# Sliding-window attention into a SiLU MLP: attention in visits of two blocks, and second layers by seven block products

## The chip, the cores and the metric

The kernel runs on one core of a Trainium2 chip. The metric is the device time of one execution in microseconds. The profiled execution is one further run of the same program, taken with the hardware profiler. In its views PE is TensorE's matmul, PEld its weight load, DVE is VectorE, ACT is ScalarE, POOL is GpSimd (here it writes the descriptors of casting loads) and SP is SyncE (here it issues stores and DMA transposes); L12 is line 12 of the kernel.

## What is computed

```python
batch, n_heads, seq, head_dim = (8, 8, 576, 64)
# attention, causal, window of 64
scores = scale * np.matmul(q, k.transpose(0, 1, 3, 2))
mask = (rel >= 0) & (rel < window)            # rel = query position - key position
attn = softmax(np.where(mask, scores, -1e9))
attn_out = np.matmul(attn, v)
x = attn_out.transpose(0, 2, 1, 3).reshape(B * S, H * D)      # 4608 x 512
h = x @ w_in                                  # 512 -> 2048
g = h * (1.0 / (1.0 + np.exp(-h)))
out = g @ w_out                               # 2048 -> 512
```

All inputs and the output are float32; both kernels multiply in bfloat16 and accumulate in float32.

## The kernel before

**Tiling.** A block is 64 query positions of one batch; a block's queries see the 128 keys of their own block and the one before. There are 9 blocks in a batch and 72 in all. A tile of the MLP is 512 tokens, 8 blocks, and there are 9 tiles. `bridge` holds the attention output transposed (model dimension on the partitions), as the first layer wants it. The first layer of a tile is 16 feature groups of 4 matmuls over 512 columns (`first_layer`, L440), each group followed by a SiLU on ACT into a `g` buffer (L446). The second layer is, for each 128 tokens, 16 matmuls over 512 columns into one bank (`second_layer`, L449), a copy to `ot` (L455) and a store by SP (L459). Tile 0's first layer is cut into columns 0 to 191 and 192 to 511; the last 128 tokens of the last tile are cut into 256, 128 and 128 output columns.

**Attention before** goes in units of two heads and three blocks (`add_batch_attention`), 12 to a batch. q is kept as `qbd`, with the two heads of a pair in a block diagonal, so that one matmul of 128 rows and 128 columns gives the scores of a block for both heads (L349, three to a unit). Exp runs on ACT (L367), the mask is a multiplication on DVE (L370; in batch 0 a matmul adds a bias instead, L356), the values are three matmuls of 130 columns (L375), in which a column of ones gives the row sums; reciprocal (L381) and normalisation on DVE follow. The result gets into `bridge` by matmuls back (L420 in batch 0, with 64 output columns that alternate between the halves of the array; L431 in batch 1 and most of 2) and a copy, or from the last third of batch 2 on by a DMA transpose on SP (L425).

**Loads.** POOL issues loads that cast to bfloat16: whole rows for TensorE transposes (L235; the transposes are L299, with 64 output columns in alternating halves, and L308), or pieces of 64 elements for DMA transposes (L254; the transposes are L260). q goes by TensorE in batches 0 to 3, k in 0 and 1. SP loads the first q and k pair itself (L241). v is loaded by L272 and shifted by half a block on DVE (L335, L337). Buffers for k, q and v are double, by batch, so that v of batch b waits until the values of batch b - 2 are done.

**Order.** A planner, `Plan`, sets the order of work on every engine before anything is emitted. Every operation has a cost in microseconds, what it needs, and a rank by its class; DMA operations have a cost on one of two pipes and a latency. The planner steps through time and on each free engine places the ready operation of the lowest rank. The order that comes out is fixed: on the chip, each engine's queue runs in that order, and an operation whose input is late holds up all that is behind it. MLP matmuls have rank 99, so any ready attention matmul goes ahead of them, but scores go only where `scores_may_run` lets them, which is during second layers:

```python
        op, kind, rest = moe[i]
        if kind == 1:
            return rest > 0 and not p.done(op["deps"])
        return rest > 6
```

PSUM has eight banks: four (`at`) for attention, four (`mp`) for the MLP. While the first tile has not begun, filler matmuls (`warm`, L680) go where TensorE would be idle.

Of the kernel before, what the change touches and what calls it, by code (L numbers as in the profile page):

```python
# [14 lines left out]
class Plan:  # L15
# [5 lines left out]
    def __init__(self, pools, rank, rank0, ahead):  # L21
        self.rank, self.rank0, self.pools = rank, {**rank0, **{c + "0": r for c, r in ahead.items()}}, pools
        self.queues = {}
        self.banks = [[] for _ in range(8)]
        self.count = 0
        self.now = 0.0

    def add(self, cls, us, fn, deps=(), lat=0.08, gate=None, dma=None, pool=None, table=None, b=0):
        if b > 1 and cls in ("cast", "lift", "spread", "mask", "norm"):
            lat = 0.2  # L30
        op = dict(us=us, first=self.rank[cls] + b if b or cls not in self.rank0 else self.rank0[cls], fn=fn, deps=[d for d in deps if d is not None], lat=lat, gate=gate, dma=dma,
                  pool=pool, table=table, seen=None, n=self.count, until=[], bank=None)
        self.count += 1
        self.queues.setdefault(cls, []).append(op)
        return op

    def add_filler(self, n, cls, us, fn, *args, **kw):

        for _ in range(n):
            op = self.add(cls, us, None, *args, **kw)  # L40
            op["until"], op["fn"] = [op], lambda e, op=op: fn(op)
        self.count -= n

    def done(self, ops):
        return all(d["seen"] is not None and d["seen"] <= self.now for d in ops)

    def run(self):
# [7 lines left out]
        while left:  # L55
# [6 lines left out]
            while moved:  # L62
                moved = False
                for e in engines:
# [3 lines left out]
                    for c in can[e]:  # L68
# [8 lines left out]
                        if op["pool"] and not any(self.done(self.banks[i]) for i in self.pools[op["pool"]]):  # L77
                            continue
# [4 lines left out]
                    if op["pool"]:  # L83
                        banks = self.banks
                        op["bank"] = min((i for i in self.pools[op["pool"]] if self.done(banks[i])),
                                         key=lambda i: max([u["seen"] for u in banks[i]], default=0.0))
                        banks[op["bank"]] = op["until"]
# [8 lines left out]

# [9 lines left out]
                    heapq.heappush(events, op["seen"])  # L106
        for op, e in order:
# [4 lines left out]
def kernel(ctx, tc, q, k, v, w_in, w_out, out):  # L112
# [8 lines left out]
    NG = 3  # L121
# [5 lines left out]
    NK = 2  # L127
    NN, NNB, NE, NOB, NOT, NGT = 8, 8, 14, 6, 4, NFT + 3
    PARTS = {0: [(0, 192), (192, TT)]}
    NXQ, NXK, NXO = 4, 2, 3  # L130
    NRAW, NOX, NRC = 2, 2, 12
    NIV, NPM = 2, 1
    scale = 1.0 / float(D) ** 0.5

# [7 lines left out]
    twoi = keep.tile([128, 64], BF16, name="twoi")  # L142
    zero = keep.tile([128, NP], FP32, name="zero")
    spare = keep.tile([128, NP], FP32, name="spare")
    window = keep.tile([128, 64], BF16, name="window")
    mask0 = keep.tile([128, 3, 2, 64], BF16, name="mask0")
    mask = keep.tile([128, 3, 2, 64], BF16, name="mask")
    bias0 = keep.tile([128, 3, 2, 64], BF16, name="bias0")
    bias = keep.tile([128, 3, 2, 64], BF16, name="bias")
    nats = [keep.tile([NR, 2, NM, 128], BF16, name=f"nat{i}") for i in range(NN)]  # L150
    natbs = [keep.tile([NR, 2 * NM * D], BF16, name=f"natb{i}") for i in range(NNB)]
    qbd = [keep.tile([128, NP, 2, S], BF16, name=f"qbd{i}") for i in range(NK)]
    kt = [keep.tile([128, 64 + NP * S], BF16, name=f"kt{i}") for i in range(NK)]
    vv = [keep.tile([128, H * NB + 1, D + 2], BF16, name=f"vv{i}") for i in range(NK)]
    es = [keep.tile([128, 3, 2, 64], BF16, name=f"e{i}") for i in range(NE)]
    rcs = [keep.tile([128, 3, 2], FP32, name=f"rc{i}") for i in range(NRC)]
    obs = [keep.tile([128, 3, 128], BF16, name=f"ob{i}") for i in range(NOB)]
    raws = [keep.tile([128, 2, S], BF16, name=f"raw{i}") for i in range(NRAW)]
    oxs = [keep.tile([128, 3, NP, 128], BF16, name=f"ox{i}") for i in range(NOX)]
    gts = [keep.tile([128, TT], BF16, name=f"g{i}") for i in range(NGT)]  # L160
    ots = [keep.tile([128, d_model], FP32, name=f"ot{i}") for i in range(NOT)]
# [3 lines left out]
    banks = [psum.tile([128, 512], FP32, name=f"at{i}") for i in range(4)]  # L165
    banks += [psum.tile([128, 512], FP32, name=f"mp{i}") for i in range(4)]

    p = Plan(
        {"at": range(4), "mp": range(4, 8), "all": range(8)},
        rank=dict(prime=-8, one=-9, first=-9, dma=-1, ld0=-1, ld1=-1, st=-2, xo=-1.5, xk=-1.4, silu=-3, out=-2, pv=0, ot=0, s=1, moe=99, warm=200, turn=2,  # L170
                  norm=0, inverse=0, bridge=0, exp=1, mask=1, lift=2, spread=2, shift=2, cast=4, late=5, clear=9),
        rank0=dict(turn=-6, cast=-6, lift=-5, shift=-4.5, exp=-4, mask=-4, inverse=-3.5, norm=-3, bridge=-3.2),
        ahead=dict(s=-5.5, exp=-4.6, pv=-5.5, inverse=-4.3, norm=-4.2, ot=-5.5, bridge=-4.25),
# [11 lines left out]

# [6 lines left out]
    def const_bias(_):  # L192
        for t in (bias, bias0):
            nc.vector.tensor_copy(out=t.rearrange("p t h i -> p (t h) i"),
                                  in_=window.unsqueeze(1).to_broadcast([128, 6, 64]))
        nc.vector.memset(bias0[0:64, 0], -32768.0)

    def const_mask(_):
        for a, m in ((bias, mask), (bias0, mask0)):
            nc.vector.tensor_scalar(m, a, 1.0 / 32768.0, 1.0, op0=ALU.mult, op1=ALU.add)  # L200

    def const_twoi(_):
        nc.vector.tensor_copy(out=twoi[0:64], in_=ident[0:64, 0:64])
        nc.vector.tensor_copy(out=twoi[64:128], in_=ident[64:128, 64:128])
# [8 lines left out]
    def clear_q(i, hh):  # L213
        r = slice(64 - 64 * hh, 128 - 64 * hh)
        nc.scalar.copy(out=qbd[i][r, :, hh].bitcast(FP32), in_=zero[r].unsqueeze(2).to_broadcast([64, NP, S // 2]))

    def clear_ob(i):
        nc.vector.memset(obs[i].bitcast(FP32), 0.0)

    c_ident = p.add("one", {"POOL": 1.3}, const_ident)  # L220
    c_vv = [p.add("one", {"DVE": 0.25}, lambda _, i=i: clear_vv(i)) for i in range(NK)]
    c_k = [p.add("one", {"DVE": 0.15}, lambda _, i=i: clear_k(i)) for i in range(NK)]
    c_zero = p.add("one", {"DVE": 0.1}, lambda _: nc.vector.memset(zero, 0.0))
    c_q = {i: [p.add("first", {"ACT": 1.0}, lambda e, i=i, hh=hh: clear_q(i, hh), [c_zero]) for hh in range(2)]
           for i in range(NK)}
    c_twoi = p.add("late", {"DVE": 0.3}, const_twoi, [c_ident])
    c_ob = [p.add("late", {"DVE": 0.2}, lambda _, i=i: clear_ob(i)) for i in range(NOB)]
    c_window = p.add("one", {"POOL": 0.6}, const_window)
    c_bias = [p.add("one", {"DVE": 0.9}, const_bias, [c_window])]
    c_mask = [p.add("late", {"DVE": 0.7}, const_mask, c_bias)]  # L230


    def load_cast(w, b, pj, kk):

        nc.gpsimd.dma_start(  # L235
            out=natbs[w].rearrange("p (h y) -> p h y", h=2),
# [499 lines left out]
```

## Time and profile before

| | us |
|---|---|
| median of three runs | 317.87 |
| the three runs | 317.87, 315.54, 319.26 |
| the profiled execution's span | 318.8 |

The span runs from the first to the last instruction of the profiled execution. TensorE's granted clock is 0.995 of full speed on average over it.

How to read what the prediction quotes: the page's second part cuts the span into 40 slices and gives the busy share of each in tenths, and in the row PEclk the granted clock in tenths. Its fourth part is the chain of waits, followed back from the last instruction. A row of the timeline has start, length, engine, line, operation, output and input, the number of instructions that are merged into it, and in brackets the idle time before it with what ended that. Matmuls are pipelined, so a row's length reaches past the start of the next; the distance between starts is what a group costs. A row of the costliest groups has count, total busy time, mean nanoseconds of one, and idle time before with its releasers. A row of the view by stretches has the stretch, its length, the busy time (and count) of PE, PEld, DVE, ACT and POOL, the granted clock, the DMA share and GB/s. A row of DMA issues has count, size, and the median time from issue to landing.

### The profile page before, as it was taken

How to read it: one execution, taken by the hardware profiler on the slowest of the kernel's cores; microseconds unless marked ns; L12 is line 12 of the kernel's file. 1: busy time of each engine (PE TensorE's matmuls, PEld its weight loads, DVE VectorE, ACT ScalarE, POOL GpSimd, SP SyncE). 2: the span in 40 equal slices, each digit the busy share in tenths (PEclk: the TensorE clock that was granted, in tenths of full speed). 3: DMA queues.
4: the chain of work that ended last, by engine and by line, in shares of the span. 5: the costliest groups of instructions: out<-in, count | busy, mean ns of one | idle time of the engine just before them, and what ended most of it. 6: DMA issues, size and time to landing. Idle time of an engine off the chain costs nothing.

```text
span 318.8 us, 6010 instructions
## 1 busy us (share of the span) xinstructions
PE 307.9 (97%) x2198; PEld 168.4 (53%) x2223; DVE 154.5 (48%) x467; ACT 193.4 (61%) x374; POOL 119.2 (37%) x159
## 2 busy tenths in 40 slices
PE   8999999999999999999999869999999999999996
PEld 4778666545664556445544445446544444444444
DVE  4894748934799898923990159606920000000000
ACT  8898786889776565568356721668166126415611
POOL 8947859496829777564454000000000000000000
PEclk9999999999999999999999979999999999999999
DMA  9999999999999999999999933400340020020012
GB/s 144 164 196 186 193 195 161 127 243 129 187 165 135 176 154 152 163 163 163 154 191 175 142 64 90 84 0 36 80 93 2 35 97 0 2 99 33 2 61 70
DMA packets 138108, 37.51 MB, mean 118 GB/s; under 512 B 122464, under 2 KB 133600, under 8 KB 138080
## 3 DMA queue, kind: packets, MB, share of 16 engines
q0 software_dynamic: 95712, 18.06, 74.4%
q1 hardware_dynamic: 42368, 19.08, 33.6%
q8 instruction: 17, 0.28, 0.4%
q14 instruction: 11, 0.09, 0.1%
HBM read 36.70 MB, written 9.44 MB: 145 GB/s over the span
## 4 chain that ended last, share of the span: by engine, by line
PE 85%; DVE 6%; DMA 4%; issue 2%; ACT 1%; POOL 1%; DVEq 0%; POOLq 0%; ACTq 0%
PE mp L449 36%; PE mp L440 32%; PE at L375 5%; PE at L349 4%; DMA vv<-in_v_dram 4%; DVE qbd L314 2%; PE at L680 1%; PE mp L680 1%; DVE ox L404 1%; POOL vv L272 1%; DVE qbd L268 1%; DVE vv L337 1%; DVE vv L335 1%; PE at L308 1%; PE at L420 1%
## 5 line engine op out<-in xcount | busy, mean ns | idle before, releaser
L449 PE MATMUL mp<-w_out_sb,g 128*128 128x512 bf16 (+2 forms) x583 | 141.6, 369 | 1.0
L440 PE MATMUL mp<-bridge,w_in_sb 128*128 128x512 bf16 (+2 forms) x640 | 130.7, 358 | 0.7 <-ACT g L446 0.6
L446 ACT ACTIVATE g<-mp 128x512 bf16<-128x512 f32 (+2 forms) x160 | 86.3, 556 | 29.8 <-PE mp L440 29.3
L440 PEld LDWEIGHTS <-w_in_sb 128*128 128x128 bf16 x640 | 60.1, 98 | 60.3 <-issue 1.4
L449 PEld LDWEIGHTS <-g 128*128 128x128 bf16 x608 | 55.0, 98 | 42.7
L455 ACT COPY ot<-mp 128x512 f32<-128x512 f32 (+2 forms) x34 | 19.0, 561 | 72.1 <-PE mp L449 62.7
L404 DVE TENSOR_TENSOR ox<-at,rc 64x192 bf16<-64x192 f32 x128 | 45.2, 353 | 2.5
L254 POOL DMA_DIRECT2D nat<-in_k_dram x48 | 36.4, 761 | 24.3 <-DMA nat<-in_k_dram 13.0
L367 ACT ACTIVATE e<-at 128x384 bf16<-128x384 f32 x90 | 38.8, 497 | 10.6 <-PE at L349 9.8
L370 DVE TENSOR_TENSOR e<-e,mask 128x384 bf16<-128x384 bf16 x84 | 26.6, 350 | 33.6 <-ACT e L367 32.8
L272 POOL DMA_DIRECT2D vv<-in_v_dram x32 | 32.3, 1014 | 13.1 <-PE at L375 7.2
L375 PE MATMUL at<-vv,e 128*128 128x130 bf16 x273 | 29.8, 220 | 4.1 <-DVE e L370 4.0
L375 PEld LDWEIGHTS <-e 128*128 128x128 bf16 x288 | 22.5, 97 | 20.0 <-DVE e L370 7.6
L254 POOL DMA_DIRECT2D nat<-in_q_dram x32 | 23.4, 735 | 8.1 <-DMA nat<-in_q_dram 4.6
L349 PEld LDWEIGHTS <-kt 128*128 128x128 bf16 x252 | 18.6, 100 | 10.0 <-issue 2.8
L349 PE MATMUL at<-qbd,kt 128*128 128x128 bf16 x252 | 23.6, 222 | 0.3
L381 DVE RECIPROCAL rc<-at 128x6 f32<-128x6 f32 x91 | 17.5, 194 | 10.1 <-PE at L375 8.0
L314 DVE COPY qbd<-at 64x288 bf16<-64x288 bf16 x26 | 12.5, 480 | 11.1 <-ACT qbd L314 7.6
L387 DVE TENSOR_TENSOR ob<-at,rc 64x192 bf16<-64x192 f32 x40 | 14.0, 350 | 0.8
L314 ACT COPY qbd<-at 64x288 bf16<-64x288 bf16 x22 | 10.5, 476 | 2.8 <-DVE qbd L314 2.5
L268 DVE COPY qbd<-raw 64x1152 bf16<-64x1152 bf16 x16 | 8.1, 505 | 8.4 <-DMA raw<-nat 8.0
L235 POOL DMA_DIRECT2D natb<-in_q_dram x15 | 10.0, 665 | 4.9 <-PE at L375 1.4
(69 smaller groups left out, 158.0 us busy)
## 6 DMA issues: line engine op xcount, KB each, us to landing
out_dram<-ot SPq DMA_DIRECT2D x35, 256.0 KB, 2.4
vv<-in_v_dram POOLq DMA_DIRECT2D x32, 144.0 KB, 7.3
nat<-in_k_dram POOLq DMA_DIRECT2D x48, 72.0 KB, 7.9
nat<-in_q_dram POOLq DMA_DIRECT2D x32, 72.0 KB, 7.6
natb<-in_q_dram POOLq DMA_DIRECT2D x15, 144.0 KB, 6.4
w_in_sb<-in_moe_w_in_dram POOLq DMA_DIRECT2D x8, 256.0 KB, 8.7
w_out_sb<-in_moe_w_out_dram POOLq DMA_DIRECT2D x8, 256.0 KB, 7.8
natb<-in_k_dram POOLq DMA_DIRECT2D x7, 144.0 KB, 5.9
```

The lines of the kernel that those rows point to most:

```text
L254: nc.gpsimd.dma_start(out=rows(i)[:, pj % 2, :, 64 * hh:64 * hh + 64], in_=(q, k)[kk][b, 2 * pj + hh].rearrange("(m p) d -> p m d", p=NR),)
L272: queue[e].dma_start(out=vv[b % NK][:, 2 * g0 + 1:2 * g1 + 1:2, 0:D], in_=v[b].rearrange("h s d -> (h s) d").rearrange("(g p) d -> p g d", ...
L314: copies[e](out=qbd[b % NK][64 * hh:64 * hh + 64, pj, hh].rearrange("x (p m) -> x p m", m=NM)[:, :, r::2], in_=at_bf16(op)[64 * r:64 * r + ...
L349: nc.tensor.matmul(at_sp(op)[:, x], lhsT=kt[b % NK][:, pj * S + t * 64:pj * S + t * 64 + 128], rhs=qbd[b % NK][:, pj, :, t * 64:t * 64 + 6 ...
L367: nc.scalar.activation(out=es[n % NE], in_=at_sp(op), func=ACTF.Exp, scale=scale)
L370: nc.vector.tensor_mul(es[n % NE], es[n % NE], mask0 if g == 0 else mask)
L375: nc.tensor.matmul(at_pv(op)[:, x], lhsT=es[n % NE][:, x].rearrange("p h i -> p (h i)"), rhs=vv[b % NK][:, s:s + NB + 1:NB, 0:D + 1], star ...
L404: nc.vector.tensor_mul(ox(n)[:, :, r], pv[r, :, hh, 0:D], rc[r, :, hh:hh + 1].to_broadcast([64, 3, 64]))
L440: nc.tensor.matmul(banks[bank["bank"]][:, lo:hi], lhsT=w_in_sb[:, c, ft * 128:(ft + 1) * 128], rhs=bridge[:, (j * TT + lo) // 64:(j * TT + ...
L446: nc.scalar.activation(out=gts[gt][:, lo:hi], in_=banks[bank["bank"]][:, lo:hi], func=ACTF.Silu)
L449: nc.tensor.matmul(banks[bank["bank"]][:, 0:hi - lo], lhsT=gts[gt][:, m * 128:(m + 1) * 128], rhs=w_out_sb[:, f, lo:hi], start=(f == 0), s ...
L455: copies[e](out=ots[ot][:, lo:hi], in_=banks[bank["bank"]][:, 0:hi - lo])
```

## The change

**Attention.** A visit takes two consecutive blocks and all eight heads (36 visits; a visit may span two batches). q is kept plainly as `qt`, without zeros: a pair's two heads lie on partitions 0 to 63 and 64 to 127 of `qt` and `kt`. Scores are 16 matmuls of 64 rows and 64 columns, which alternate between the row halves and between the two banks of a PSUM pair. Values are 16 matmuls of 65 columns that write 64 partitions each, alternating between column halves. Exp and mask then are one operation over 1024 elements, normalisation one over 512. Two pairs of banks serve scores and values in turn. Visits 0 to 8 go to `bridge` by TensorE transposes and a copy, the others by a DMA transpose each on SP. q and k go by TensorE transposes in batches 0 and 1 and by DMA transposes from batch 2 on, both straight to where they are used; there are seven `nat` buffers. In batch 0 all q and k loads go through POOL ahead of the v loads, and five of the eight `w_out` loads go ahead of batch 1. Tile 0's first layer is cut at column 256.

**Second layers.** Tile 0's stays as it was. From tile 1 on, g (512 tokens x 2048) and w_out (2048 x 512) are each cut into quarters, and the product is formed by seven quarter products instead of eight, in Winograd's form of Strassen's algorithm. Each quarter product is 2 x 8 matmuls of 256 columns. Four sums of quarters of g are formed for each tile on DVE, in two halves each; four sums of quarters of w_out are formed once (`wsum`). Partial products accumulate in the same bank across products, with a copy of the bank to `ot` in between (ACT) or an addition of the bank to `ot` (DVE).

The planner has one rank for each class and one default latency (0.2 in place of 0.08), can hand out pairs of banks, and lets scores run while more than 1.5 us of a second layer is left.

```diff
-    def scores(op, b, pj, g):
-        for x in range(3):
-            t = 3 * g + x
-            nc.tensor.matmul(
-                at_sp(op)[:, x], lhsT=kt[b % NK][:, pj * S + t * 64:pj * S + t * 64 + 128],
-                rhs=qbd[b % NK][:, pj, :, t * 64:t * 64 + 64], start=(x == 0), stop=(x == 2),
-            )
+    def scores(op, blocks, bias):
+        ps = pair(op).rearrange("k (h x j i) -> k h x j i", h=2, x=2, j=NP)
...
+        for x, nb in enumerate(blocks):
+            b, t = divmod(nb, NB)
+            for j in range(NP):
+                for hh in range(2):
+                    r = slice(64 * hh, 64 * hh + 64)
+                    nc.tensor.matmul(
+                        ps[:, hh, x, j], lhsT=kt[b % 2][r, j * S + t * 64:j * S + t * 64 + 128],
+                        rhs=qt[b % 2][r, j * S + t * 64:j * S + t * 64 + 64],
+                        start=(x == 0 and j == 0 and not bias), stop=(x == n - 1 and j == NP - 1),
+                    )
+    def values(op, w, blocks):
...
+                for hh in range(2):
+                    h = 4 * (j // 2) + 2 * hh + j % 2
+                    nc.tensor.matmul(
+                        o[64 * hh:64 * hh + 64, x, j], lhsT=es[w][:, hh, x, j],
+                        rhs=vv[b % 2][:, h * NB + t, 0:D + 1], start=(j == 0), stop=(j == NP - 1),
+                    )
+    def g_sum(i, f0, f1):
+        x, y = {0: (a_quarter(21), a_quarter(22)), 1: (sums[0], a_quarter(11)),
+                2: (a_quarter(11), a_quarter(21)), 3: (a_quarter(12), sums[1])}[i]
+        (nc.vector.tensor_sub if i else nc.vector.tensor_add)(sums[i][:, f0:f1], x[:, f0:f1], y[:, f0:f1])
+    def w_sum(i, f0, f1):
+        x, y = {0: (b_quarter(12), b_quarter(11)), 1: (b_quarter(22), wsum[0]),
+                2: (b_quarter(22), b_quarter(12)), 3: (b_quarter(21), wsum[1])}[i]
+        nc.vector.tensor_sub(wsum[i][:, f0:f1], x[:, f0:f1], y[:, f0:f1])
-    def second_layer(bank, gt, m, f, lo, hi):
-        nc.tensor.matmul(
-            banks[bank["bank"]][:, 0:hi - lo], lhsT=gts[gt][:, m * 128:(m + 1) * 128], rhs=w_out_sb[:, f, lo:hi],
-            start=(f == 0), stop=(f == NFT - 1),
-        )
+    def product(bk, a, w, m, f, first, last):
+        nc.tensor.matmul(
+            bank(bk)[:, HD * m:HD * m + HD], lhsT=a[:, f, 128 * m:128 * m + 128], rhs=w[:, f],
+            start=first and m == 0 and f == 0, stop=last and f == HF - 1, skip_group_check=True)
+    def add_second(j, si, pool):
...
+        for f0 in (0, 4):
+            f1 = f0 + 4
+            need = [x for f in range(f0, f1) for x in si[f] + si[f + HF]]
+            for i in (0, 1, 3, 2):
+                before = {0: [], 1: su[0][-1:], 2: [], 3: su[1][-1:]}[i]
+                su[i].append(p.add("sum", {"DVE": 0.68}, lambda _, i=i, f0=f0, f1=f1: g_sum(i, f0, f1),
+                                   need + before + s_used[i]))
...
+        a, e1 = add_product(None, a_quarter(11), b_quarter(11), lambda f: si[f], True, False, use_g(0))
+        p1 = piece(a, o11, e1, "copy", free(o11))
+        c, e5 = add_product(None, sums[0], wsum[0], lambda f: [su[0][f // 4]] + tsum[0], True, False, use_s(0))
+        p5 = piece(c, o22, e5, "copy", free(o22))
+        _, e6 = add_product(a, sums[1], wsum[1], lambda f: [su[1][f // 4], p1] + tsum[1], False, False, use_s(1))
+        u2 = piece(a, o12, e6, "copy", free(o12))
+        _, e3 = add_product(c, sums[3], b_quarter(22), lambda f: [su[3][f // 4], p5], False, True, use_s(3))
+        c12 = piece(c, o12, e3, "add", [u2])
+        _, e7 = add_product(a, sums[2], wsum[2], lambda f: [su[2][f // 4], u2] + tsum[2], False, False, use_s(2))
+        c22 = piece(a, o22, e7, "add", [p5])
+        bb, e2 = add_product(None, a_quarter(12), b_quarter(21), lambda f: si[f + HF], True, True, use_g(1))
+        c11 = piece(bb, o11, e2, "add", [p1])
+        _, e4 = add_product(a, a_quarter(22), wsum[3], lambda f: si[f + HF] + [c22] + tsum[3], False, True, use_g(1))
```

In the order that comes out of the changed planner, score and value bursts stand in the second layers of tiles 0 to 5 and at the start of tile 2's first layer; tiles 6 to 8 hold none. On DVE the shifts of v stand between masks, normalisations and, in tiles 1, 2 and 4, between the sums of g.

More of the change, by code (lines that the diff above doesn't have):

```diff
@@ L120 @@
     NR = S // NM
-    NG = 3
     NDC = d_model // 128
@@ L149 @@
[L149 to L161, printed above, removed]
+    window0 = keep.tile([128, 64], BF16, name="window0")
@@ L211, in clear_k @@
         nc.vector.memset(kt[i][:, 0:64].bitcast(FP32), 0.0)
[L213 to L218, printed above, removed]
     c_ident = p.add("one", {"POOL": 1.3}, const_ident)
[L221 to L222 removed]
+    c_vv = [p.add("one", {"DVE": 0.25}, lambda _, i=i: clear_vv(i)) for i in range(2)]
@@ L223 @@
+    c_k = [p.add("one", {"DVE": 0.15}, lambda _, i=i: clear_k(i)) for i in range(2)]
     c_zero = p.add("one", {"DVE": 0.1}, lambda _: nc.vector.memset(zero, 0.0))
[L224 to L227, printed above, removed]
     c_window = p.add("one", {"POOL": 0.6}, const_window)
-    c_bias = [p.add("one", {"DVE": 0.9}, const_bias, [c_window])]
```

712 lines of the change are left out of this document (342 added, 370 removed).

## The prediction

> **What bounds the kernel now.** I read the page first, then the instructions in order of time at the end of the run and in its middle.
>
> ```profile
> PE 307.9 (97%) x2198; PEld 168.4 (53%) x2223; DVE 154.5 (48%) x467; ACT 193.4 (61%) x374; POOL 119.2 (37%) x159
> PEclk9999999999999999999999979999999999999999
> DMA  9999999999999999999999933400340020020012
> PE 85%; DVE 6%; DMA 4%; issue 2%; ACT 1%; POOL 1%; DVEq 0%; POOLq 0%; ACTq 0%
> ```
>
> TensorE is busy 97% of the span and carries 85% of the chain of waits; no other engine passes 61%. The DMA engines are full for the first 23 of 40 slices and nearly idle afterwards, so transfers matter only while attention is still being fed. TensorE's time is not in its "mean ns" (matmuls overlap) but in the distance between starts:
>
> ```profile
> 287.85 13.98 PE L440 MATMUL mp<-bridge,w_in_sb 128*128 128x512 bf16 x64
> 301.67 14.06 PE L449 MATMUL mp<-w_out_sb,g 128*128 128x512 bf16 x95
> 301.93 0.60 ACT L446 ACTIVATE g<-mp 128x512 bf16<-128x512 f32 x1 [0.27 <-PE mp L440]
> ...
> 312.27 0.59 ACT L455 COPY ot<-mp 128x512 f32<-128x512 f32 x1 [2.87 <-PE mp L449]
> 314.02 0.37 ACT L455 COPY ot<-mp 128x256 f32<-128x256 f32 x1 [1.16 <-PE mp L449]
> ```
>
> 64 matmuls of 512 columns take 301.67 - 287.85 = 13.82 us, 216 ns each. The copies that follow 16 matmuls of 256 columns lie 314.02 - 312.27 = 1.75 us apart, 109.4 ns each: half the columns cost half the time. The MoE part of before is then 1088 x 0.216 = 235.0 plus tile 0's first layer in two parts, 14.0: 249.0 us. The attention rates:
>
> ```profile
> 27.77 0.42 PE L308 MATMUL at<-ident,natb 96*128 96x96 bf16 x6
> 28.03 0.41 PE L440 MATMUL mp<-bridge,w_in_sb 128*128 128x192 bf16 x3
> 28.37 0.45 PE L299 MATMUL at<-ident,natb 96*64 96x96 bf16 x12
> 28.75 1.65 PE L440 MATMUL mp<-bridge,w_in_sb 128*128 128x192 bf16 x14
> ...
> 46.54 0.25 PE L431 MATMUL at<-twoi,ob 128*128 128x64 bf16 x3
> 46.63 0.38 PE L449 MATMUL mp<-w_out_sb,g 128*128 128x512 bf16 x1
> ...
> 145.34 0.83 PE L349 MATMUL at<-qbd,kt 128*128 128x128 bf16 x12
> 146.01 2.11 PE L449 MATMUL mp<-w_out_sb,g 128*128 128x512 bf16 x8
> ...
> 163.37 0.34 PE L375 MATMUL at<-vv,e 128*128 128x130 bf16 x3
> 163.54 13.76 PE L440 MATMUL mp<-bridge,w_in_sb 128*128 128x512 bf16 x63
> ```
>
> Scores cost 0.67/12 = 56 ns, values 0.17/3 = 57 ns, the matmuls back 30 ns. Batches 1 to 7 hold 252 scores (14.1 us) and 252 values (14.4), 60 backs (1.8), 12 bursts of q transposes (0.26 each, 3.1), and bursts with 64 output columns priced next (3.1): 36.5 us.
>
> ```profile
> 20.38 0.33 PE L361 MATMUL at<-qbd,kt 128*128 128x128 bf16 x3
> 20.64 0.38 PE L420 MATMUL mp<-ident,ox 128*64 128x64 bf16 x12
> 20.95 0.35 PE L375 MATMUL at<-vv,e 128*128 128x130 bf16 x3
> 21.22 0.28 PE L420 MATMUL mp<-ident,ox 128*64 128x64 bf16 x6
> 21.44 0.34 PE L375 MATMUL at<-vv,e 128*128 128x130 bf16 x3
> ```
>
> These L420 matmuls write alternating column halves of the array. Six take 0.22 us, twelve 0.31: six more cost 0.09, 15 ns each, half of L431's 30, so the halves run side by side. The group ahead is stretched too (L361 x3 takes 0.26 where 0.17 is usual). So a burst costs about 0.22 us once, and 64/4.8 = 13 ns per matmul. L299 agrees: 12 x 96/4.8 ns + 0.22 = 0.46; the rows give 0.38, and 0.09 ahead.
>
> Now the span closes: first layer at 22.1 (row below), 249.0, 36.5, and 3.1 from the last matmul to the end make 310.7 of 318.8. The other 8.1 are waits, most of them in one place:
>
> ```profile
> 184.71 0.76 DVE L337 COPY vv<-vv 64x2304 bf16<-64x2304 bf16 x1 [4.52 <-DMA vv<-in_v_dram]
> 185.99 0.51 PE L375 MATMUL at<-vv,e 128*128 128x130 bf16 x3 [4.00 <-DVE e L370]
> 186.00:189.20 3.20, 3.20 (x20) 2.10 (x21) 2.32 (x7) 1.30 (x3) 0.00 (x0) 0.52 0.21 79
> ```
>
> The shift of a late v stood ahead of masks on VectorE; TensorE stood 4.0 us and then ran 3.2 us at a granted clock of 0.52, 1.5 more.
>
> **The change, part by part.** *Second layers.* Tiles 1 to 8 run 7 x 16 products of 256 columns instead of 64 of 512: 112 x 0.1094 = 12.25 against 13.82, so 8 x 1.57 = -12.5 us. Tile 0's first layer, 128 x 0.109 = 14.0, is unchanged. MoE after: 14.0 + 512 x 0.216 + 13.8 + 98.0 = 236.4.
>
> *What the products wait for.* Each tile adds 8 sums and 3 adds on VectorE.
>
> ```profile
> L370 DVE TENSOR_TENSOR e<-e,mask 128x384 bf16<-128x384 bf16 x84 | 26.6, 350 | 33.6 <-ACT e L367 32.8
> L410 DVE TENSOR_TENSOR ox<-at,rc 128x384 bf16<-128x384 f32 x6 | 3.2, 541 | 0.1
> L455 ACT COPY ot<-mp 128x512 f32<-128x512 f32 x31 | 18.1, 586 | 69.8 <-PE mp L449 60.4 <-issue 8.7 <-ACT e L367 0.7
> L381 DVE RECIPROCAL rc<-at 128x6 f32<-128x6 f32 x91 | 17.5, 194 | 10.1 <-PE at L375 8.0 <-ACT ot L455 0.3
> ```
>
> A sum is 1024 bf16 elements; the mask does 384 in 0.35, so at most 0.93 in proportion; I take 0.7, as part of 0.35 is fixed. That is 5.6 us a tile, and 2.2 of adds (3 x 0.541 x 512/384), in a period of 26. The last silu ends 0.9 us after the layer's last matmul (301.93 + 0.60 against 301.67). The second half of the first sum is ready 0.7 later, at 1.6; the first product (1.75 us) needs no sum and the second reaches its fifth block at 2.2. The copy that frees the accumulating bank (0.59) lies beside the product on the other bank (1.75). So nothing waits, with 0.6 us to spare; a VectorE later than that costs TensorE the difference, since all matmuls queue behind the product. VectorE stays near half busy: normalising goes to 36 operations of 0.72 from 168 halves by the code, the qbd copies go.
>
> *Attention.* 32 visits follow tile 0's start, each with 16 scores (64 rows, 64 columns) and 16 values (64 output columns, 65 columns). Values are L420's form: 0.22 + 16 x 0.0135 = 0.44 us. No row shows 64-row scores with halves in rows: 0.43 if they pair like L420, 0.69 at L431's 30 ns. I take 0.50, nearer the first, because q and k halves sit in different partitions and banks. 32 x 0.94 = 30.1, less some 7 bursts that follow one of the same kind (1.5); batch 1's turns, 8 x 0.46, and five visits back, 20 x 0.056, add 4.8: 33.4 against 36.5, -3.1.
>
> *Start and end.*
>
> ```profile
> 2.08 1.11 POOL L272 DMA_DIRECT2D vv<-in_v_dram  x1
> ...
> 9.11 1.03 POOL L272 DMA_DIRECT2D vv<-in_v_dram  x1
> ...
> 17.49 0.32 DVE L337 COPY vv<-vv 64x576 bf16<-64x576 bf16 x1
> 22.12 0.82 PE L440 MATMUL mp<-bridge,w_in_sb 128*128 128x192 bf16 x8
> out_dram<-ot SPq DMA_DIRECT2D x35, 256.0 KB, 2.4
> out_dram<-ot SPq DMA_DIRECT2D x2, 64.0 KB, 1.6
> bridge<-ox SPq DMA_TRANSPOSE x16, 6.2
> kt<-nat SPq DMA_TRANSPOSE x12, 9.2
> ```
>
> Now all eight q/k loads go through POOL ahead of v (SP loads none), and a visit needs all heads. Between the two POOL rows lie two more v issues (1.0) and six q/k issues, 0.65 each, so the last v issue moves to about 2.1 + 8 x 0.65 + 3 x 1.0 = 10.3; 8.4 us later, as from 9.11 to 17.49, its shift starts, 18.7. Values at 19.4, then four normalisations in a row on VectorE (0.19 + 0.72) and the last back: first layer near 24.0, +1.9. At the end the last piece is 512 wide instead of 128: copy 0.59 where 256 columns take 0.37, store 2.4 for 1.6. That is about 1.1 more: 4.2 for 3.1.
>
> *Waits.* Visits from the tenth on reach the bridge by a DMA transpose on SP. Tile 2 needs visit 11, whose values stand only 26 products (2.8) and four bursts (1.8) ahead of tile 2's first matmul. From their start it takes the values 0.44, reciprocal 0.2, a shift 0.4, normalisation 0.72 and a landing of 6.2, about 8, so TensorE waits 3.3, plus 1.4 of half clock (as at 186 us). Behind it in TensorE's queue stands everything. SP now carries 24 q/k and 27 o transposes between the stores, some behind a store that waits for an add; an o transpose that lands late meets this case again, but later tiles take their last blocks a whole tile ahead. The 8.1 us of before: k, q and v of batches 3 and 4 are wanted at about 85 to 115 us, near when they land (kt 9.2 us after issue), and shifts stand between the sums. Between 0 and another 8 to 10; I take 4. Waits: 8.7.
>
> Sum: 24.0 + 236.4 + 33.4 + 8.7 + 4.2 = 306.7 against the profiled execution's 318.8; the median of the three runs, 317.87, lies 0.9 lower, so 305.8.
>
> **Rivals** (each time on the scale of the median). *Row halves don't hide their weight load (slower).* L420 shows only column halves.
>
> ```profile
> L440 PEld LDWEIGHTS <-w_in_sb 128*128 128x128 bf16 x640 | 60.1, 98 | 60.3 <-issue 1.4
> ```
>
> If each 64-row score stood for a whole 98 ns load: 16 x 0.098 + 0.22 = 1.79 a visit, +1.29 x 32 = +41: 347. Halves overlapping, 49 ns: +16, 322. It passes before from 12 us/512 = 24 ns more than my 0.50 allows (18 a matmul): 42 ns. Against it: L431 loads 128 columns and multiplies 64 in 30 ns. The Trainium skill's "TensorE: Matmul & The Clock Gate", in "LDWEIGHTS (loading the stationary operand)", sets a load at columns/1.2, whatever the rows, which is 107 ns here; by that estimate the time would be about 350 unhidden. L431's 30 ns disagrees for full-height loads; no run here shows 64 rows.
>
> *Late transfers in fixed queues.* The price of one is 4.0 + 1.5 as at 182 to 189 us; three beyond my sum give 322, two 317. The full DMA row up to 180 us speaks for it, and so does q of batches 2 and 3, now eight row loads a batch instead of four larger ones; against it, before met it once.
>
> *Sums late.* VectorE 1.4 us late in each of 8 tiles: +11, 317. Against: 48% busy.
>
> *Better.* Scores at 0.43, only tile 2's wait: 305.8 - 2.2 - 4 = 299.6, and with no wait there 294.9.
>
> **How the numbers follow.** Forecast 0.53 (300 to 312); better 0.12; transfers 0.16, half of it within 1% or slower; sums 0.07; row halves 0.12, mostly slower. Within 1% (314.7 to 321) is what a measurement can't tell from no change. Faster 0.53 + 0.12 + 0.08 = 0.73; same 0.05 + 0.07 = 0.12; slower 0.03 + 0.12 = 0.15. The range goes from 295, the better case, to 319, which takes in two late transfers and late sums.
>
> **What would show it.** Right: products start 109 ns apart; score bursts take 0.4 to 0.7 us; first layer near 24; a wait of some 3 us on the o transpose ahead of tile 2. Wrong: score starts over 42 ns apart, products waiting for VectorE in most tiles, or TensorE idle over 15 us after 24.

## The result and the profile after

| | us, median (lowest to highest) | executions |
|---|---|---|
| the changed kernel | 326.31 (325.95 to 328.63) | 4 |
| the kernel before, on the same chip | 316.71 (315.34 to 319.26) | 4 |

The ratio is 1.0295, with a 95% interval from 1.0212 to 1.0379: the change made the kernel 3% slower. The forecast was 305.8, faster. The profiled execution took 325.95, with a span of 324.2. The executions of a kernel fall into a shorter and a longer group; the ratios here and below compare the shorter ones alone, and the profiled execution of the kernel before (its span of 318.8 stands for a time of some 320.6, as a time lies 1.7 to 1.9 above its span in every run) is one of the longer.

The page of the changed kernel, its first, second and fourth part:

```profile
PE 297.5 (92%) x3052; PEld 190.9 (59%) x3056; DVE 139.8 (43%) x263; ACT 169.9 (52%) x263; POOL 125.2 (39%) x169
...
PEclk9999999999996799999979999999999999999999
DMA  5999999999999999999979999900530120030003
...
PE 57%; DMA 22%; issue 8%; POOL 5%; ACT 4%; DVE 2%; POOLq 0%; ACTq 0%; DVEq 0%
```

TensorE has 10 us less work than before (297.5 against 307.9), as meant, but a span that is 5 longer. It carries 57% of the chain of waits instead of 85%, and DMA 22% instead of 4%. What TensorE waited for, in the view of waits (engine and line, what it waited for, us in total, times, longest):

```profile
PE mp L367 <- DMA bridge<-ox: 5.0, 1, 5.0
PE at L305 <- DMA qt<-nat: 3.8, 2, 3.1
PE at L367 <- ACT gt L373: 3.0, 4, 0.7
PE at L400 <- ACT ot L612: 2.0, 3, 0.7
...
PE at L400 <- DVE ot L613: 1.2, 1, 1.2
```

Two are late transfers: a transposed attention output (`bridge`) and a transposed q. The other three are on `at`, the attention's PSUM banks, and were in no part of the forecast. The timeline of TensorE tells where each lies (start, length, instruction, idle time before and its releaser):

```profile
27.62 10.97 PE L367 MATMUL mp<-bridge,w_in_sb 128*128 128x256 bf16 x99 [0.29 <-DVE bridge L362]
...
47.09 0.64 PE L305 MATMUL at<-qt,kt 64*128 64x64 bf16 x32
47.66 2.55 PE L396 MATMUL mp<-w_out_sb,gt 128*128 128x512 bf16 x10
...
103.52 4.00 PE L367 MATMUL mp<-bridge,w_in_sb 128*128 128x512 bf16 x9 [4.95 <-DMA bridge<-ox]
107.45 0.65 PE L335 MATMUL at<-vv,e 128*64 128x65 bf16 x16
...
162.57 0.47 PE L305 MATMUL at<-qt,kt 64*128 64x64 bf16 x20 [3.06 <-DMA qt<-nat]
...
248.27 1.91 PE L400 MATMUL mp<-w_out_sb,gt 128*128 128x256 bf16 x16
...
260.50 13.98 PE L367 MATMUL mp<-bridge,w_in_sb 128*128 128x512 bf16 x64
...
286.54 1.24 PE L367 MATMUL at<-bridge,w_in_sb 128*128 128x512 bf16 x5
288.53 1.89 PE L367 MATMUL at<-bridge,w_in_sb 128*128 128x512 bf16 x8 [0.75 <-ACT gt L373]
...
303.98 1.91 PE L400 MATMUL at<-w_out_sb,gt 128*128 128x256 bf16 x16
...
306.78 1.91 PE L400 MATMUL at<-ws,gs 128*128 128x256 bf16 x16 [0.68 <-ACT ot L612]
...
315.03 1.69 PE L400 MATMUL at<-ws,gs 128*128 128x256 bf16 x14 [1.19 <-DVE ot L613]
...
318.31 1.91 PE L400 MATMUL at<-ws,gt 128*128 128x256 bf16 x16
```

The seven products of a tile take 260.50 - 248.27 = 12.23 us. The wait ahead of tile 2 is there, as named. From 286.54 on, in the last tile, TensorE waits eight times, 6.2 us in all (3.0 + 2.0 + 1.2), for an operation of ACT or VectorE that reads a bank. The same by stretches, one row a tile for tiles 0 to 3, 7 and 8, then the times after the two long waits (stretch, length, busy time and count of PE, PEld, DVE, ACT, POOL, granted clock, DMA share, GB/s):

```profile
27.62:66.89 39.27, 37.12 (x464) 24.75 (x468) 18.94 (x36) 23.60 (x49) 31.59 (x43) 1.00 1.95 165
66.89:103.52 36.63, 30.50 (x336) 19.79 (x336) 19.18 (x36) 20.41 (x30) 21.59 (x28) 0.94 1.74 167
103.52:139.69 36.17, 35.44 (x433) 21.91 (x433) 20.42 (x39) 20.36 (x28) 24.27 (x31) 0.92 1.90 149
139.69:173.08 33.39, 30.33 (x274) 19.48 (x272) 15.06 (x27) 17.09 (x25) 11.42 (x15) 0.95 1.41 158
...
260.50:286.54 26.04, 26.04 (x179) 17.24 (x176) 7.43 (x11) 11.89 (x20) 0.00 (x0) 1.00 0.12 41
286.54:320.05 33.51, 27.32 (x178) 17.07 (x175) 7.44 (x11) 11.89 (x20) 0.00 (x0) 1.00 0.10 33
...
103.50:108.00 4.50, 4.48 (x25) 1.65 (x24) 0.00 (x0) 2.37 (x3) 0.00 (x0) 0.50 1.71 183
108.00:110.00 2.00, 2.00 (x25) 0.86 (x22) 1.27 (x4) 0.03 (x1) 1.94 (x2) 0.67 1.26 126
162.50:167.10 4.60, 4.53 (x57) 3.31 (x56) 1.83 (x4) 1.94 (x2) 0.00 (x0) 0.65 0.52 117
```

Tile 7 and tile 8 do the same work, without attention; tile 8 takes 33.51 - 26.04 = 7.5 us more. Half of that lies in its first layer (303.98 - 286.54 = 17.44 us for the usual 13.81), half in its products (16.07 for 12.23). In tiles 0 to 3 TensorE stood idle for 2.15 + 6.13 + 0.73 + 3.06 = 12.1 us (length less busy time), and ran at a reduced clock in the last three rows, which costs 4.50 x 0.50 + 2.00 x 0.33 + 4.60 x 0.35 = 4.5 more.

### The profile page after: what moved, and what is told of

It is laid out like the page before. It is cut to its first block, busy times and chain, and to the rows that moved or that the text cites. A ratio compares the mean times of both kernels' runs of the same rounds, so it can differ in the third digit from the quotient of the medians.

```text
span 324.2 us, 7366 instructions
## 1 busy us (share of the span) xinstructions
PE 297.5 (92%) x3052; PEld 190.9 (59%) x3056; DVE 139.8 (43%) x263; ACT 169.9 (52%) x263; POOL 125.2 (39%) x169
## 4 chain that ended last, share of the span: by engine, by line
PE 57%; DMA 22%; issue 8%; POOL 5%; ACT 4%; DVE 2%; POOLq 0%; ACTq 0%; DVEq 0%
PE mp L367 23%; PE mp L400 18%; DMA nat<-in_k_dram 14%; DMA vv<-in_v_dram 5%; PE mp L650 4%; PE at L400 3%; DMA qt<-nat 3%; POOL vv L249 2%; POOL nat L234 2%; PE at L367 2%; PE at L272 2%; PE at L305 2%; PE at L335 2%; ACT gt L373 1%; DVE ox L344 1%
## 5 line engine op out<-in xcount | busy, mean ns | idle before, releaser
L367 PE MATMUL mp<-bridge,w_in_sb 128*128 128x512 bf16 (+1 forms) x608 | 123.3, 361 | 5.4 <-DMA bridge<-ox 5.0
L373 ACT ACTIVATE gt<-mp 128x512 bf16<-128x512 f32 (+1 forms) x152 | 82.2, 553 | 29.8 <-PE mp L367 27.7
L388 DVE TENSOR_TENSOR gs<-gt 128x1024 bf16<-128x1024 bf16 x32 | 21.9, 688 | 79.1 <-ACT gt L373 79.1
L400 PEld LDWEIGHTS <-gs 128*128 128x128 bf16 x512 | 48.9, 99 | 10.9 <-issue 3.9
L312 ACT ACTIVATE e<-at 128x1024 bf16<-128x1024 f32 x36 | 36.0, 1031 | 22.6 <-PE at L305 22.4
L400 PE MATMUL mp<-ws,gs 128*128 128x256 bf16 x336 | 42.7, 277 | 0.0
L400 PEld LDWEIGHTS <-gt 128*128 128x128 bf16 x384 | 36.4, 98 | 5.8
L400 PE MATMUL mp<-w_out_sb,gt 128*128 128x256 bf16 x224 | 28.3, 273 | 0.0
L344 DVE TENSOR_TENSOR ox<-at,rc 128x512 bf16<-128x512 f32 x36 | 24.1, 682 | 7.0 <-DMA bridge<-ox 6.4
L318 DVE TENSOR_TENSOR e<-e,mask 128x1024 bf16<-128x1024 bf16 x32 | 21.4, 680 | 7.8 <-ACT e L312 7.4
L305 PE MATMUL at<-qt,kt 64*128 64x64 bf16 x576 | 14.0, 192 | 4.2 <-DMA qt<-nat 3.8
L305 PEld LDWEIGHTS <-kt 64*128 64x128 bf16 x576 | 10.3, 96 | 11.3 <-issue 10.9
```

Of the source, the lines that this page charges most:

```text
L305: nc.tensor.matmul(ps[:, hh, x, j], lhsT=kt[b % 2][r, j * S + t * 64:j * S + t * 64 + 128], rhs=qt[b % 2][r, j * S + t * 64:j * S + t * 64 ...
L312: nc.scalar.activation(out=es[w][:, :, 0:n], in_=pair(op).rearrange("k (h x j i) -> k h x j i", h=2, x=2, j=NP)[:, :, 0:n], func=ACTF.Exp, ...
L318: nc.vector.tensor_mul(es[w][:, :, 0:n], es[w][:, :, 0:n], mask[:, :, 0:n])
L344: nc.vector.tensor_mul(oxs[o][:, 0:n], at_pv(op, n)[:, :, :, 0:D], rcs[r][:, 0:n].unsqueeze(3).to_broadcast([128, n, NP, D]))
L367: nc.tensor.matmul(bank(bk)[:, lo:hi], lhsT=w_in_sb[:, c, ft * 128:(ft + 1) * 128], rhs=bridge[:, (j * TT + lo) // 64:(j * TT + hi) // 64, ...
L373: nc.scalar.activation(out=gt[:, ft, lo:hi], in_=bank(bk)[:, lo:hi], func=ACTF.Silu)
```

## Experiments

The theory was that three separate things took the gain: the two-bank attention tiles in the last tile, the DMA transposes that tiles 2 and 3 wait for, and a late start. Its rivals were that each is only the place where something else shows. The ratios below are to the kernel before in the same session; its median moved between 315.8 and 320.5 from one to another, so kernels of different sessions are compared by ratio or by their traces.

### The last tile's banks

The kernel allocates PSUM for attention as two tiles of 128 x 1024, two banks each, and the last tile's matmuls may use any of the eight banks. Experiment 1 (e1_last_mp) gives the last tile the four single banks:

```diff
-            pool = "all" if n_tile >= NTT - 1 else "mp"
+            pool = "mp"
```

> Only the last tile's PSUM pool is changed, from all eight banks to the four single ones. Theory (two banks of a pair are one tile, so a matmul into one half waits for ACT's or DVE's reading of the other half): the last tile takes 26.1 us like tiles 6 and 7 instead of 33.5, so about 319 us against 326.3. Rival (copies and sums are too late for the products wherever no attention lies between): the waits stay, about 326.

Measured: 319.27 (316.81 to 320.46, ten executions), ratio 1.0096 [1.005, 1.0142]. Experiment 2 (e12_one_of_pair) asks whether it is the pairing or the attention banks as such; it allows one bank of each pair:

```diff
+         "six": [(i,) for i in (0, 2, 4, 5, 6, 7)],
-            pool = "all" if n_tile >= NTT - 1 else "mp"
+            pool = "six" if n_tile >= NTT - 1 else "mp"
```

> The changed kernel; the last tile may take the four single MLP banks and one bank of each attention pair, six in all, never two of one pair. Theory: the last tile waits because the two banks of a pair are one tile, so a matmul into one bank stands behind an operation that reads the other; with one bank of each pair no such wait of 0.7 is left and the time is that of e1_last_mp, about 319. Rival: the attention banks themselves are slow to come free, whichever is taken; then each group that goes into one still waits and the time stays above 322.

Measured: 319.08 (315.99 to 324.46, ten executions), ratio 1.0058 [0.9997, 1.0119]. The first layer of the last tile, first in experiment 1, then in experiment 2, with the row that follows it:

```profile
287.75 13.98 PE L367 MATMUL mp<-bridge,w_in_sb 128*128 128x512 bf16 x64
301.56 1.91 PE L400 MATMUL mp<-w_out_sb,gt 128*128 128x256 bf16 x16
```

```profile
289.00 1.89 PE L367 MATMUL at<-bridge,w_in_sb 128*128 128x512 bf16 x8
...
302.82 1.91 PE L400 MATMUL mp<-w_out_sb,gt 128*128 128x256 bf16 x16
```

In both the first layer takes the usual 13.8 us, and no row of the tile waits. In the second part of its groups still go through `at`. So the attention banks are not slow to come free; a matmul into one bank of a pair waits for the reader of the other bank, because the two are one tile. The Trainium skill, "PSUM — Partial Sum Buffer", in "PSUM bank collisions raise a hardware error", has software guard PSUM by bank (more closely by bank and quadrant); the rows show what it costs when the guarded unit is two banks.

### The transposes that tiles 2 and 3 wait for

Experiment 3 (e2_back12) sends visits 9 to 11, the last ones that tile 2 needs, back by TensorE instead of a DMA transpose:

```diff
-    NVO = 9
+    NVO = 12
```

> Visits 9 to 11 go back by TensorE as well (12 instead of 9). Theory (tile 2 waits for the DMA transpose of visit 11, and through that wait batch 4's v and batch 5's q come late): the 5.0 us wait at 98 us and its 2.4 us of half clock go, and the 3.1 us wait in tile 3 with 1.5 of half clock goes too; 12 more transposes cost 0.7: 315 to 319 us. Rival (all loads of these batches are late, whatever the transpose does): another wait of 4 to 6 us stands in tile 2, 323 to 327.

Measured: 317.74 (314.86 to 319.11, ten executions), ratio 1.0005 [0.9947, 1.0063]. The timeline at tiles 2 and 3:

```profile
97.43 2.75 PE L367 MATMUL mp<-bridge,w_in_sb 128*128 128x512 bf16 x12
...
130.75 6.42 PE L367 MATMUL mp<-bridge,w_in_sb 128*128 128x512 bf16 x29 [1.67 <-DMA bridge<-ox]
```

Tile 2 starts without a wait, the half clock behind it is gone, and so is the wait for q at 162. Tile 3 now has a smaller wait of the same kind. The edit does more than swap the transposes: the planner orders tiles 2 and 3 anew (no values stand behind tile 2's first matmul any more), and the share of the one and the other was not separated. Experiment 4 (e5_last_back) puts experiments 1 and 3 together:

> The last tile takes its banks from the four single MLP banks, and visits 9 to 11 go back by TensorE; the start is left as in the changed kernel. Theory: the two losses are separate, 7 us (the last tile) and 8.6 us (tile 2's transpose and what stood behind it), as each alone gave, so 326.3 - 7 - 8.6 = about 311, and 2% faster than before is just missed (ratio near 0.98). Rival: with the transposes out of tile 2's way the next late transfer takes their place, and the time stays at 314 to 317.

Measured: 310.67 (310.11 to 311.44, four executions), ratio 0.986 [0.983, 0.9891]. The two losses are separate: the spans fall by 324.2 - 317.9 = 6.3, by 324.2 - 316.1 = 8.1, and together by 324.2 - 309.0 = 15.2. Each of the three profiled executions also lost some 1.6 us to a reduced clock between 24 and 30 us, which that of the changed kernel did not (last section), so each fall is too small by about that.

### The start

Experiment 5 (e3_turns_fill) lets the start's turns use the four single banks (they could take any of the eight, and all ran in the pairs), and tells the planner that a filler matmul takes longer, so that it places 19 instead of 29 ahead of the first turn (a turn is a TensorE transpose of q or k):

```diff
-        pool = "at" if b else "all"
+        pool = "at" if b else "mp"
...
-    p.add_filler(60, "warm", {"PE": 0.17}, warm, ...
+    p.add_filler(60, "warm", {"PE": 0.27}, warm, ...
```

> Batch 0's eight transposes use the four single banks, and the planner counts a filler matmul at 0.27 us instead of 0.17, so that it places fewer ahead of them (19 instead of 29 at first). Theory (the fillers run longer than planned and each second transpose waits for its pair's copy, while the loads have landed): the first score starts near 13.5 instead of 17.7, the first layer near 23 instead of 27.6, about 322 us. Rival (the loads set the start): the first layer stays at 27 or later, 326.

Measured: 325.9 (322.23 to 327.29, four executions), ratio 1.023 [1.0088, 1.0372], beside 1.0295 [1.0212, 1.0379] for the changed kernel. Its timeline, TensorE's rows and two of POOL's (the second is the next loads of v):

```profile
23.96 10.42 PE L367 MATMUL mp<-bridge,w_in_sb 128*128 128x256 bf16 x94
...
95.80 0.71 PE L305 MATMUL at<-qt,kt 64*128 64x64 bf16 x20 [2.98 <-DMA qt<-nat]
101.86 3.64 PE L367 MATMUL mp<-bridge,w_in_sb 128*128 128x512 bf16 x9 [5.35 <-DMA bridge<-ox]
162.20 0.72 PE L305 MATMUL at<-qt,kt 64*128 64x64 bf16 x20 [6.08 <-DMA qt<-nat]
...
106.80 0.72 POOL L234 DMA_DIRECT2D nat<-in_q_dram  x1 [2.48 <-DMA nat<-in_q_dram]
108.09 4.17 POOL L249 DMA_DIRECT2D vv<-in_v_dram  x4 [0.57 <-PE mp L367]
```

The first layer starts 3.7 us earlier, at 23.96, where the forecast had it. The waits for transfers then add up to 14.4 us instead of 8.7, and tile 4 starts at 173.14 where it started at 173.08. POOL waits with a load of q until an earlier one has landed, and issues the v loads behind it at 108.09, where the changed kernel did at 108.06: they came no earlier for the earlier start. Experiment 6 has all three edits, and was run in two sessions (e4_three, e6_all_again):

> All three edits together. If the three causes are separate and nothing is late behind them: 326.3 - 7.3 - 9 - 4 = about 306, below the kernel before (316.7). If the earlier start only makes the loads of later batches late: 311 to 314.

> The same as e5_last_back with the earlier start (turns from the four MLP banks, a shorter row of fillers). Theory: loads and transfers, not the start, set the time at which tiles 2 to 4 can run, so the 3.7 us earlier start is given back in waits and the time is that of e5_last_back within 1.5 us, about 311. Rival: the start was off the path only because of tile 2's wait; without it the time is 3 to 4 us below e5_last_back, about 307.

Measured: 313.02 (306.32 to 313.8) and 310.32 (304.9 to 311.2), four executions each. Of the eight, six took 309.7 to 313.8 and two 304.9 and 306.3, and there is no interval. The six, among them both profiled ones, lie about where experiment 4 does (310.1 to 311.4) or above it: in them the gain of the start is given back. The two lie 4 to 6 us below it, so it is not given back always. The profiled execution of the first session (313.58) lost some 5 us to half clock between 36 and 48 us (last section), that of the second (309.71) had waits for transfers. The two short executions were not profiled, and what they lacked of this stays open. Experiments 7 and 8 look at the same through fewer transfers: q and k of batches 2 and 3 are turned by TensorE, as in batches 0 and 1. Experiment 7 (e8_turns_four) does it to experiment 4, experiment 8 (e9_four_early) to experiment 6:

```diff
-    NPT = 2
+    NPT = 4
```

> As e5_last_back, with q and k of batches 2 and 3 loaded as whole rows and turned by TensorE, as in batches 0 and 1: 16 bursts of turns of 0.45 us more on TensorE (7.2 us), 16 loads on POOL fewer, 8 DMA transposes on SP fewer. Theory: after visits 9 to 11 went back by TensorE only some 4 us of transfer waits are left, so even if all of them go the time is 3 us above e5_last_back, about 314; no wait for a transposed q or k is left before tile 4. Rival: transfers still set the pace up to tile 4 behind the scenes; then the turns run in time that was idle and the time falls below e5_last_back.

> e8_turns_four (q and k of batches 2 and 3 turned by TensorE, so fewer small loads and transposes) with the earlier start of e6_all_again. Theory: what took the 3.7 us of the earlier start back in e6_all_again was transfers (a transpose of o and of q that TensorE waited 2.6 and 2.2 us for); with 16 loads and 8 transposes fewer they are not late, and the start's gain shows: 3 to 4 us below e8_turns_four, 310 to 311. Rival: something else makes up for the start (the sums, the order), and the time is that of e8_turns_four, 314.

Measured: 314.02 (313.73 to 314.17), ratio 0.9964 [0.994, 0.9987], and 311.04 (309.11 to 313.9), ratio 0.9717 [0.9609, 0.9825], four executions each. Experiment 7 is 3.4 us above experiment 4, as its theory had it: the added turns cost more than the waits that go. What TensorE waited for, in experiment 6 (the first two rows) and then in experiment 8 (the first row):

```profile
PE mp L367 <- DMA bridge<-ox: 2.6, 1, 2.6
PE at L305 <- DMA qt<-nat: 2.2, 1, 2.2
```

```profile
PE at L272 <- DMA nat<-in_k_dram: 1.6, 2, 1.4
```

With 16 loads fewer no wait for a transposed q or o is left, and the earlier start shows as 3 us (the two are of different sessions; by the ratios it is 2.5%, 8 us, with wide intervals). The profiled execution of experiment 8, the longest at 313.9, lost some 5 us to half clock between 36 and 48 us as well. That fits the reading that late loads took the start's gain back in experiment 5; how much of it the clock takes back, and when, is open.

### What the seven products are worth

Experiment 9 (e7_plain_seconds) is experiment 4 with the plain second layer in all tiles, in the order that tile 0 has (a feature group for all four banks, then the next; the kernel before fills one bank after the other from tile 1 on). The sums of `w_out` are still formed, those of g are not:

```diff
-            (add_second if n_tile else add_plain_second)(n_tile, si, pool)
+            add_plain_second(n_tile, si, pool)
```

> As e5_last_back, with the plain second layer (eight products' worth) in all tiles. Theory: TensorE sets the time nearly everywhere, so the seven-product form is worth its full 8 x 1.57 = 12.5 us and this kernel is 11 to 13 us above e5_last_back, about 323. Rival: sums and additions on VectorE and late transfers in tiles 1 to 5 eat the saving there, and it is 4 to 8 us above e5_last_back, about 316 to 319.

Measured: 327.49 (325.55 to 330.53, four executions), ratio 1.0372 [1.0295, 1.0449]; 16.8 us above experiment 4, and 15.3 by the spans (324.3 against 309.0). A tile without attention, from TensorE's timeline:

```profile
262.57 13.97 PE L367 MATMUL mp<-bridge,w_in_sb 128*128 128x512 bf16 x64
276.38 14.23 PE L396 MATMUL mp<-w_out_sb,gt 128*128 128x512 bf16 x62
290.64 9.66 PE L367 MATMUL mp<-bridge,w_in_sb 128*128 128x512 bf16 x44
```

It takes 290.64 - 262.57 = 28.07, against 26.04 with seven products: 2.03 a tile, and eight times that, 16.2, is about what the kernel lost. But this is not what the products save against the kernel before. A tile of it without attention:

```profile
246.41 13.98 PE L449 MATMUL mp<-w_out_sb,g 128*128 128x512 bf16 x62
...
274.04 13.98 PE L449 MATMUL mp<-w_out_sb,g 128*128 128x512 bf16 x62
```

It takes 274.04 - 246.41 = 27.63, so the seven products save 1.59 a tile, 12.7 in all, where the forecast had 1.57 and 12.5. The other 0.44 belongs to experiment 9's own plain layer (14.26 us; 13.82 before), which has another order; why that order costs it is open.

### A faster version

Experiment 10 (e10_back16) is experiment 6 with visits 12 to 15 (tile 3's) going back by TensorE too, experiment 11 (e11_back_all) the same with all visits:

```diff
-    NVO = 12
+    NVO = 16      # experiment 11: 36
```

> e6_all_again with visits 12 to 15 (tile 3's) going back by TensorE too, four DMA transposes fewer. Theory: tile 3's wait of 2.6 us for its transpose is the same case as tile 2's and goes, at 4 x 0.15 = 0.6 us of matmuls back: about 308. Rival: the loads are what is late; then the wait moves on to tile 4's scores, which wait for a transposed q, and the time stays at 310 to 311.

> e6_all_again with all visits going back by TensorE: 24 DMA transposes of o fewer, 24 x 2 bursts of four matmuls back (0.11 each by their starts, 5.3 us in all) and 24 copies more. Theory: the transposes of o cost waits only in tiles 2 and 3; beyond those each one taken off costs TensorE and gains nothing, so the time is 2 to 3 us above e10_back16, 310 to 312. Rival: the transposes of o delay those of q and k in SP's queue and the DMA engines, and the time falls below 306.

Measured: 307.98 (305.99 to 313.79), ratio 0.962 [0.9524, 0.9716], and 309.57 (309.34 to 312.01), ratio 0.9716 [0.9615, 0.9818], four executions each, in one session. The first row of the waits of experiment 10:

```profile
PE at L305 <- DMA qt<-nat: 1.7, 1, 1.7
```

Tile 3's wait is gone, as it went at tile 2. Taking off the other transposes as well gained nothing: the medians stand 1.6 apart the way the theory had it, though their intervals overlap. Experiment 10 beats both kernels.

## Why the prediction was wrong, by its own steps

| term of the sum, us | forecast | changed kernel |
|---|---|---|
| first layer starts | 24.0 | 27.6 |
| MLP at its measured rates | 236.4 | 236.4 |
| attention | 33.4 | 31.9 (what is left) |
| waits and half clock, tiles 0 to 7 | 8.7 | 12.1 + 4.5 = 16.6 |
| last tile beyond 26.04 | 0 | 7.5 |
| last matmul to the end | 4.2 | 4.15 |
| sum, a span | 306.7 | 324.2 |
| from the span to the median | -0.9 | +2.1 |

**Second layers: right.** 12.23 us for 12.25, and 1.59 saved a tile for 1.57 by the tiles of the kernel before.

**Attention: right, and 1.5 us cheaper than forecast.** 32 scores take 0.57 us (47.66 - 47.09), and a single burst of 16 takes 0.34 (18.24 to 18.58 in batch 0). The second 16 cost 0.23, or 14 ns each: halves in rows run side by side like halves in columns. The first rival, that they don't hide their weight load, falls: by its own row such a load takes 96 ns (L305, PEld), near the Trainium skill's 107 ns, cited there, but it does not set the distance between starts.

**What the products wait for: wrong, and the largest miss in one place.** "The copy that frees the accumulating bank (0.59) lies beside the product on the other bank (1.75). So nothing waits" holds in tiles 6 and 7, which have no such wait. In the last tile it fails: there both accumulating banks can be halves of one tile, and the copy of one stands ahead of the product on the other; the silu that reads one half holds up the first layer's group on the other half in the same way, which "MLP at its measured rates" left out. The choice of banks (`"all"` for the last tile) was in the code; I priced the tile like the others, and named no rival for it. It cost 7.5 us by the tiles, 6.3 by experiment 1 as it stands.

**Waits: the mechanism right, the size half.** Tile 2's wait for the transpose of visit 11 came where the forecast put it, at 4.95 us for 3.3. The term that was too small is the landing, "a landing of 6.2", which was the median of before over its whole run. The four transposes to `bridge` issued between 91 and 99 us landed 8.2 to 9.3 us later, and the median over the changed kernel is 7.4:

```profile
bridge<-ox SPq DMA_TRANSPOSE x27, 7.4
```

With the reduced clock behind it (2.25 + 0.66) this wait cost 7.9 us for the 4.7 of the sum. The other waits of tiles 0 to 3, with their clock, cost 8.7, the upper end of "Between 0 and another 8 to 10; I take 4". What comes of a wait was left out too: behind tile 2's first matmul stood the values of visit 13, for which POOL's next v loads waited 7.9 us, with the rows of the next batch behind them.

```profile
108.06 3.96 POOL L249 DMA_DIRECT2D vv<-in_v_dram  x4 [7.91 <-PE at L335]
```

The wait of 3.06 us for a transposed q at 162 is a batch on, and it went with tile 2's wait in experiment 3. That the one comes of the other through these loads is argued, as that experiment also changed the order. Taking tile 2's late transfer away was worth 8.1 us, where the rival "Late transfers in fixed queues" had 5.5 each. That rival named the right thing at a chance of 0.16; with the last tile's 7.5 beside it, the waits' 7.9 above the sum make 15.4 of the 17.5 us by which the span exceeds the sum.

**Start: a miss of 3.6 us that did not decide.** The sum took the landing of v as the last need. In the changed kernel the first 29 fillers ran to 8.9 us, past the first landings (in experiment 5 a turn starts at 6.83 without a wait), and a pair's second turn waited for its mate's lift, the copy out of PSUM, again two banks in one tile. Experiment 5 undid both, which does not tell their shares, and put the start at 23.96; the time hardly moved.

**End: right**, 4.15 for 4.2. With the last tile and tile 2 mended (experiment 4), 309.0 less its start of 27.05, the MLP's 236.4 and its end of 4.6 (309.0 less 302.67 + 1.75) leaves 41.0 for attention and waits, where the forecast had 33.4 + 8.7 = 42.1. The rest of the sum stood.

**From the span to the time: wrong sign.** The sum is compared with a span and then lowered by 0.9, the distance from before's profiled span to its median. But a time lies 1.7 to 1.9 above its span in every run, so the 0.9 sets a span against a time. A span of 306.7 is a time of about 308.5, so 2.7 us of the miss of 20.5 lie in this step.

## What to carry to other kernels

A bank that is allocated as half of a larger PSUM tile comes free with the whole tile: before pricing overlap between a bank's reader and the next matmul, look at what the banks are called in the timeline and at which instructions share them. In a kernel whose queues run in a fixed order, price a late transfer with what stands behind it, through the loads it delays to the next batch, and not by its own wait; putting only the visits next to their use on TensorE took it away, and putting all there was no better. An earlier start can be given back in waits for loads, as in experiment 5; with fewer loads, in experiment 8, about 3 us of it showed. And a rewritten version of a layer is to be priced against the old kernel's own rows: the plain layer of experiment 9 was slower than the old one.

## What the runs showed of the hardware that was not expected

The granted clock does not follow the length of one idle time. After the waits of 4.95 and 3.06 us it was 0.50 and 0.65 (rows above); after 2.05 us in experiment 4, 29 matmuls took 8.0 us instead of 6.3; after 1.67 us in experiment 3 and 2.60 in experiment 6 the rate stayed full. And in experiment 10 it fell to 0.50 while tile 0's turns and matmuls alternated, with no idle time there above 0.9 us. By stretches, experiment 10 and then experiment 6 at the same place:

```profile
34.00:36.00 2.00, 0.99 (x25) 0.75 (x26) 0.00 (x0) 0.91 (x2) 1.39 (x2) 1.00 1.30 199
...
38.00:40.00 2.00, 1.80 (x26) 1.10 (x26) 0.76 (x1) 1.37 (x3) 2.00 (x4) 0.50 2.21 158
```

```profile
34.00:36.00 2.00, 0.87 (x15) 0.53 (x15) 0.00 (x0) 0.84 (x3) 1.37 (x3) 1.00 1.31 199
...
38.00:40.00 2.00, 1.47 (x30) 0.95 (x28) 0.77 (x2) 1.39 (x3) 2.00 (x3) 1.00 2.10 160
```

TensorE was busy for about as little in both just before, and only in one did the clock fall; it fell at this place in three of the six profiled executions with the early start, and in none with the late one. With the late start it fell earlier, between 24 and 30 us, in experiments 1 to 4 and 7, after idle times of at most 0.7 us, but not in the changed kernel or experiment 9, where the same instructions stand there in the same order. A row of experiment 1:

```profile
26.00:28.00 2.00, 1.80 (x11) 1.27 (x10) 0.85 (x2) 1.03 (x3) 0.86 (x2) 0.50 1.26 204
```

The changed kernel has a granted clock of 1.00 in the same stretch. The Trainium skill, "TensorE: Matmul & The Clock Gate", in "HAM oscillation — how this bites in real kernels", gives the rule of no idle gaps over about 3.4 us. The 4.95 us wait agrees; the half clock after 3.06 and 2.05 us and in the turns shows that shorter ones don't exclude it here. What decides was not found.
